# Scores of odd attention blocks in the banks of the first layer's products, seven weight-splitting pieces after step 12, attention's pools closed before the first layer's rest

## The chip, the cores and the metric

The kernel runs on one core of one Trainium2 chip. The time is device microseconds of one execution. The engines named below are TensorE (PE in the rows, its weight loads PEld), VectorE (DVE), ScalarE (ACT), GpSimd (POOL) and SyncE (SP), which issues the transfers. [...]

## What is computed

A chain of three parts. Attention with a local window of 32 positions and 32 global tokens; a first feed-forward layer (three weight matrices, the maximum over the three products, then an output matrix); and a layer of eight experts, each token going to one. Cut to what matters here:

```python
s_g = scale * q_g @ k_all.T;  out_g = softmax(s_g) @ v_all             # global queries see all
s_l = concat(scale * q_l @ k_g.T, where(|i - j| <= 32, scale * q_l @ k_l.T, -1e9))
out_l = softmax(s_l) @ concat(v_g, v_l)
x = concat(out_g, out_l)                                               # 1152 x 512
h = max(max(x @ w1, x @ w2), x @ w3)                                   # w: 512 x 768
x2 = h @ w_out
# then gate, argmax, and out[i] = gate_i * (relu(x2[i] @ W1[e]) @ W2[e])
```

## The kernel before

Attention is cut into 16 sets of two blocks, 32 blocks n of 128 queries and two heads each. A loop over steps s = -2 ... 37 runs them as a pipeline; each step does a little of several blocks. `SEQ` is the order inside a step (its first string for s < 14, its second from 14 on):

- `scores` (`u_scores(s + 2)`, L179): sixteen small matmuls into the tile `s`, two PSUM banks; `ps_s` has one such pair. In steps 1, 5, 9, 13 ... `glob` (`g_scores`, L257) writes the global queries' scores beside them, and `gcopy` (L272) copies those out.
- `max` (`u_max`, L193, on DVE): adds the mask, takes row maxima `nm` and leaves the masked scores in SBUF as `sm`. After it the pair of banks may be written again.
- `exp` (`u_exp`, L198, on ACT), `trans` (L212, `pt`, then ACT's copy `ph`, L217), `pv` (L226, `pv`, then DVE's `xq`, L228), `out` (L234, `pxq`, ACT's copy `xs`, L237, and POOL's split into `xh` and `xl`, L239 and L240). There is one bank each for `pt`, `pv` and `pxq`, so block n's product is written only after `xq` of block n - 1.
- `w0`, `w1`, `w2`: pieces of `w_stream`, the splitting of the float64 weights (18 tiles of 128 x 512 for the first layer, 6 of `w_out`) into two fp32r halves. A tile is seven pieces: ACT `ca` (L337), DVE `ca` (L339), `ca` (L342), `ct` (L345), ACT `wh` (L349), DVE `ca` (L352), DVE `ca` (L354) with POOL's two operations for `wl` (L355, L356); the next tile's load is issued along with them. `w_steps` is the number of pieces in a step: with nw pieces, `w0` gets nw // 3, `w1` (nw + 1) // 3 and `w2` (nw + 2) // 3.
- `idle`: `warm` matmuls on zeros (L88), which compute nothing; `idles` gives their number in a step. Each call takes a bank of `ps_mm`.
- `m0` ... `m3`: matmuls of the first layer (L455), pulled from `moe_stream` in the order of the table `ORDER` (window of tokens, slice of 128 of the 768 columns, and from which step on). A product is 12 matmuls into one bank of `ps_mm`, which has three; `part` then takes it out with ACT (L440), or with DVE, which keeps a running maximum `hA` (L442).

After the loop the rest of `moe_stream` runs with one piece of splitting behind every fifth matmul (the "rest" below). Then attention's pools are closed, and the banks that they held go to new pools: `BANKS`, the list that products rotate through, becomes six banks instead of three, and from there on `split64` keeps its scratch `a` in PSUM (`cap` in the rows instead of `ca`). Then come the other slices of the first layer, `w_out`, and the experts.

The instructions of each engine run in the order in which this code writes them. A set's queries and keys are a load of 320 KB, its values 512 KB, a tile of weights 512 KB, all in one queue of SP.

Of the kernel before, what the change touches and what calls it, by code (L numbers as in the profile page):

```python
# [7 lines left out]
F32 = mybir.dt.float32  # L8
# [6 lines left out]
ALU = mybir.AluOpType  # L15
# [4 lines left out]
P = 128  # L20
# [30 lines left out]
def tile_block(ctx: ExitStack, tc: tile.TileContext, qk, qg, v, vo, vg, w123, w_out, w_gate, w1, w2, consts, out):  # L51
    nc = tc.nc
# [18 lines left out]
    ps_mm = ctx.enter_context(tc.tile_pool(name="ps_mm", bufs=3, space=PSUM))  # L71
# [3 lines left out]
    ps_s = att.enter_context(tc.tile_pool(name="ps_s", bufs=1, space=PSUM))  # L75
# [17 lines left out]
    SS, raws, K, V, VG, W, SG_, PV_, PS_, PT_, SM, hT, GS = {}, {}, {}, {}, {}, {}, {}, {}, {}, {}, {}, {}, {}  # L93
# [76 lines left out]

    def u_scores(n):
        m, u = divmod(n, 2)
        ps = ps_s.tile([P, 2, 512], F32, tag="s", name=f"s{n}")
        PS_[n] = ps
        for j in range(2):
            t = K[m][64 * j : 64 * j + 64]
            for g in range(4):
                a = 256 + 32 * (5 * u + g)
                nc.tensor.matmul(ps[32 * g : 32 * g + 32, j, 0:P], lhsT=t[:, u * P + 32 * g : u * P + 32 * g + 32], rhs=t[:, a : a + P], start=True, stop=True)  # L179

    def u_max(n):
        m, u = divmod(n, 2)
        half = SETS[m][1]
        mk = mask[:, 0 if half == 0 and u == 0 else (2 if half == 1 and u == 1 else 1), :]
        nm = ap.tile([P, 2], F32, tag="nm", bufs=4, name=f"nm{n}")
        if u == 0:
            SS[m] = ap.tile([P, 2, 4], F32, tag="ssum", bufs=3, name=f"ss{m}")
        ssum = SS[m][:, 0, 2 * u : 2 * u + 2]
        sm = sms[n % NSM]
        SM[n] = (sm, nm, ssum)  # L190
        ps = PS_[n]
        for j in range(2):
            nc.vector.tensor_tensor_reduce(sm[:, j], ps[:, j, 0:P], mk, scale=-0.125, scalar=3.0e38, op0=ALU.add, op1=ALU.min, accum_out=nm[:, j : j + 1])  # L193

    def u_exp(n):
        sm, nm, ssum = SM[n]
# [46 lines left out]
    def g_scores(m):  # L243

        b, half, hp = SETS[m]
        quad = hp // 2
        if half == 0:
            SG_[b, quad] = ap.tile([P, S], F32, tag=f"sg{quad}", bufs=2, name=f"sg{b}{quad}")
        ps = PS_[2 * m + 3]
        n = 256 + 32 * half  # L250
        GS[m] = [ps[64 * j : 64 * j + 64, j, P : P + n] for j in range(2)]

        def part(out, cols):
            for a in range(2):
                for j in range(2):
                    r = slice(64 * j, 64 * j + 64)
                    nc.tensor.matmul(out(GS[m][j][32 * a : 32 * a + 32]), lhsT=QG[b][r, hp + a, 32 * j : 32 * j + 32], rhs=cols(K[m + a][r, 288:608]), start=True, stop=True)  # L257

        for s in range(2):
            part(  # L260
                lambda o: o[:, 0:256].rearrange("p (u s c) -> p u s c", u=2, s=2)[:, :, s],
                lambda k: k.rearrange("p (u c) -> p u c", u=2)[:, :, 96 * s : 96 * s + 64],
            )
        if half == 1:
            part(lambda o: o[:, 256:288], lambda k: k[:, 64:96])

    def g_copies(m):
# [309 lines left out]
    ws = w_stream()  # L577
# [2 lines left out]

    WIN1 = [(0, 256), (256, 256), (512, 288), (800, 288)]

    ORDER = [(0, 0, 13), (1, 0, 18), (0, 1, (20, 24, 26)), (2, 0, 27), (1, 1, 27), (2, 1, 27), (0, 2, (35, 35, 36)), (3, 0, 99), (1, 2, 99), (2, 2, 99), (3, 1, 99), (3, 2, 99)]

    def moe_stream():
        for g, f, at in ORDER:
            at = at if isinstance(at, tuple) else (at,) * 3
# [18 lines left out]

    SEQ = ('m3 scores glob max gcopy m2 w0 trans m1 pv out w1 recip quad exp w2 m0 idle', 'w0 trans scores glob max pv out gcopy idle exp w1 m3 m0 quad recip m1 m2 w2')
    GDVE = 6
    MM = ((3, 2, 1, 1), (7, 4, 2, 1))

    w_steps = {1: 1, 2: 2, 3: 2, 4: 2, 5: 2, 6: 2, 7: 2, 8: 2, 9: 2, 10: 3, 11: 3, 12: 2, 13: 1, 14: 1, 15: 2, 16: 2, 17: 1, 18: 2, 19: 2, 20: 2, 21: 2, 22: 2, 23: 2, 24: 2, 25: 2, 26: 2, 27: 3, 28: 2, 29: 2, 30: 3, 31: 3, 32: 3, 33: 3, 34: 2, 35: 2, 36: 2, 37: 2}
    idles = {-2: 4, 0: 1, 2: 1, 4: 3, 6: 1, 7: 1, 8: 1, 9: 2, 10: 1, 11: 1}

    GQ = {17: (0, 0), 21: (0, 1), 28: (1, 0), 31: (1, 1)}
    globs = []
    mstream = None
# [6 lines left out]
    for s in range(-2, NU + 6):  # L623
        live, ahead = 0 <= s < NU, 0 <= s + 2 < NU
        if s == 10:
            mstream = Stream(moe_stream())
        pull = (lambda n: mstream.pull(n, s)) if mstream else (lambda n: None)
        nw = w_steps.get(s, 0)
        for c_ in SEQ[0 if s < 14 else 1].split():
# [27 lines left out]
            elif c_[0] == "m" and c_ != "max":  # L657
                pull(MM[s > 26][int(c_[1])])

        if s % 2 == 0:  # L660
            m = (s + 8) // 2
# [9 lines left out]
            routing_start()  # L671
        if s == 30:
            nc.sync.dma_start(out.rearrange("(p i) (j c) -> p (i j) c", p=64, c=P), zero[0:64].unsqueeze(1).to_broadcast([64, NT * DM // 64 // P, P]))
    k = 0
    while mstream.next is not None:
        mstream.pull(1, 100)
        k += 1
        if mstream.next is not None and k % 5 == 0:
            take(ws, 1)
    flush()  # L680
    att.close()
    s2 = phl.enter_context(tc.tile_pool(name="s2", bufs=1))
    ps_x = ctx.enter_context(tc.tile_pool(name="ps_x", bufs=2, space=PSUM))
# [666 lines left out]
```

## Time and profile before

| what | value |
|---|---|
| median of three runs | 324.5 us (323.12 to 324.73) |
| the profiled execution, its own time | 324.16 us |
| its span, first to last instruction | 322.4 us, 1.8 us less than its time |
| TensorE busy | 306.5 us, 95% of the span |
| VectorE busy | 236.8 us, 73% |
| ScalarE busy | 181.6 us, 56% |
| GpSimd busy | 148.4 us, 46% |
| mean granted TensorE clock | 0.994 of full speed |

Busy shares are averages over stages with different limits. A time in the rows is counted from the first instruction of the span. In a row of the timeline the bracket at the end is the time that the engine sat idle before that instruction, and what ended it.

### The profile page before, as it was taken

What the parts mean: (1) busy time and instruction counts of PE and PEld (TensorE: products, weight loads), DVE (VectorE), ACT (ScalarE), POOL (GpSimd) and SP (SyncE); (2) the same over time, 40 slices, a digit from 0 to 9 for tenths busy, and PEclk for the clock granted to TensorE, in tenths of its full rate; (3) what the DMA queues carried; (4) which work ended last, traced back from release to release, by engine and by line L of the source; (5) the groups of instructions that cost most, each with busy time, mean ns of one, the idle gap of its engine ahead of it and who ended that gap; (6) DMA issues with size and microseconds to landing.
All of it is one profiled execution on the core that took longest, in us unless ns stands there. A gap on an engine that the chain in (4) does not pass through costs nothing. (4 is left out here: it accounts for less than half of the span.)

```text
span 322.4 us, 8727 instructions
## 1 busy us (share of the span) xinstructions
PE 306.5 (95%) x3284; PEld 260.8 (81%) x3284; DVE 236.8 (73%) x600; ACT 181.6 (56%) x457; POOL 148.4 (46%) x164
## 2 busy tenths in 40 slices
PE   7977998999999989999999999999999999999984
PEld 2544786778999989899999999999898778888852
DVE  2699577868887999999951004756787999999871
ACT  4876988786753333444331121348331789889851
POOL 1267746677694767788672000140000448731131
PEclk9999899999999999999999999999999999999999
DMA  7999887644972323332000030588564299999920
GB/s 256 412 404 401 312 297 266 234 147 149 198 201 67 103 95 93 106 130 67 0 3 0 2 130 2 176 309 323 206 212 182 79 365 399 393 403 399 383 67 22
DMA packets 27655, 64.42 MB, mean 200 GB/s; under 512 B 3018, under 2 KB 8140, under 8 KB 27600
## 3 DMA queue, kind: packets, MB, share of 16 engines
q1 hardware_dynamic: 26304, 59.91, 53.2%
q0 software_dynamic: 1296, 3.82, 3.3%
q8 instruction: 30, 0.49, 0.6%
q14 instruction: 25, 0.20, 0.2%
HBM read 60.95 MB, written 7.27 MB: 212 GB/s over the span
## 5 line engine op out<-in xcount | busy, mean ns | idle before, releaser
L455 PE MATMUL h<-xh,wh 128*128 128x256 f32 (+1 forms) x288 | 85.2, 296 | 1.7 <-DVE hA L442 1.7
L455 PE MATMUL h<-xl,wh 128*128 128x256 f32 (+1 forms) x288 | 84.3, 293 | 0.0
L455 PE MATMUL h<-xh,wl 128*128 128x256 f32 (+1 forms) x288 | 84.1, 292 | 0.0
L455 PEld LDWEIGHTS h<-xh,wh 128*128 128x128 f32 x288 | 54.9, 191 | 3.2 <-DVE hA L442 3.0
L455 PEld LDWEIGHTS h<-xh,wl 128*128 128x128 f32 x288 | 54.7, 190 | 0.6 <-issue 0.5
L455 PEld LDWEIGHTS h<-xl,wh 128*128 128x128 f32 x288 | 54.8, 190 | 0.2
L445 POOL TENSOR_TENSOR hTl<-hA,hTh 128x256 fp32r<-128x256 f32 (+1 forms) x24 | 20.4, 850 | 55.8 <-ACT hTh L444 55.8
L239 POOL CAST xh<-xs 128x128 fp32r<-128x128 f32 x32 | 14.9, 466 | 30.7 <-ACT xs L237 30.6
L749 PE MATMUL x<-hTl,wo_h 128*128 128x256 f32 (+1 forms) x96 | 28.3, 294 | 0.0
L869 DVE TENSOR_TENSOR w2l<-rawb,w2h 128x1024 fp32r<-128x1024 f32 x23 | 27.2, 1216 | 1.4 <-ACT w2h L868 1.4
L198 ACT ACTIVATE sm<-sm,nm 128x128 f32<-128x128 f32 x64 | 25.2, 398 | 4.9 <-DVE nm L193 4.8
L749 PE MATMUL x<-hTh,wo_l 128*128 128x256 f32 (+1 forms) x96 | 27.9, 291 | 0.0
L749 PE MATMUL x<-hTh,wo_h 128*128 128x256 f32 (+1 forms) x96 | 27.8, 289 | 0.0
L193 DVE CUSTOM_DVE_ANT_0 sm<-s,mask 128x128 f32<-128x128 f32 x64 | 16.0, 286 | 15.9 <-PE s L179 9.8
L442 DVE TENSOR_TENSOR hA<-hA,h 128x256 f32<-128x256 f32 (+1 forms) x48 | 20.6, 429 | 7.5 <-PE h L455 7.1
L356 POOL TENSOR_TENSOR wl<-ct,ca 128x512 fp32r<-128x512 f32 x18 | 24.7, 1370 | 2.6 <-DVE ca L354 1.4
L952 PE MATMUL py<-w2h,hhl 128*128 128x512 f32 x96 | 25.4, 395 | 0.2 <-DVE idsall L574 0.2
L869 DVE TENSOR_TENSOR w1l<-rawb,w1h 128x1024 fp32r<-128x1024 f32 x20 | 23.7, 1216 | 1.8 <-ACT w1h L868 1.7
L355 POOL TENSOR_TENSOR ct<-ct,wh 128x512 f32<-128x512 f32 x18 | 24.5, 1363 | 0.0
L349 ACT CAST wh<-ct 128x512 fp32r<-128x512 f32 x18 | 11.1, 617 | 21.9 <-DVE ct L345 21.6
L868 ACT CAST w2h<-rawb 128x1024 fp32r<-128x1024 f32 x23 | 23.3, 1048 | 0.2 <-DMA rawb<-in_w_dram 0.2
L827 POOL DMA_INDIRECT xg<-x2d,idsall x7 | 14.9, 2123 | 16.2 <-PE xp L839 15.0
(232 smaller groups left out, 719.1 us busy)
## 6 DMA issues: line engine op xcount, KB each, us to landing
rawb<-in_w_dram SPq DMA_DIRECT2D x51, 512.0 KB
raww<-in_w_dram SPq DMA_DIRECT2D x18, 512.0 KB
rawv<-in_v_dram SPq DMA_DIRECT2D x16, 512.0 KB
qk<-in_qk_dram SPq DMA_DIRECT2D x16, 320.0 KB
rawo<-in_w_out_dram SPq DMA_DIRECT2D x6, 512.0 KB
rw<-in_w_dram SPq DMA_DIRECT2D x5, 512.0 KB
out_dram<-zero SPq DMA_DIRECT2D x1, 2176.0 KB
rawg<-in_vo_dram SPq DMA_DIRECT2D x4, 512.0 KB
```

The lines of the kernel that those rows point to most:

```text
L193: nc.vector.tensor_tensor_reduce(sm[:, j], ps[:, j, 0:P], mk, scale=-0.125, scalar=3.0e38, op0=ALU.add, op1=ALU.min, accum_out=nm[:, j : j ...
L198: nc.scalar.activation(sm[:, j], sm[:, j], AF.Exp, bias=nm[:, j : j + 1], scale=-1.0, accum_out=ssum[:, j : j + 1])
L239: nc.gpsimd.tensor_copy(dst[0], xs)
L355: nc.gpsimd.tensor_tensor(tf, tf, hi.bitcast(F32), op=ALU.subtract)
L356: nc.gpsimd.tensor_tensor(lo, tf, b.bitcast(F32), op=ALU.add)
L442: nc.vector.tensor_tensor(hA[:, :T], hA[:, :T], ph[:, :T], op=ALU.max)
L445: nc.gpsimd.tensor_tensor(hl[:, f_, c0 : c0 + T], hA[:, :T], dst.bitcast(F32), op=ALU.subtract)
L455: nc.tensor.matmul(ph[:, :T], lhsT=w_[:, a], rhs=x_[:, c, c0 : c0 + T], start=n == 0, stop=n == 11)
L749: nc.tensor.matmul(po[:, :T], lhsT=w_[:, f, d * P : (d + 1) * P], rhs=h_[:, f_, c0 : c0 + T], start=k == 0, stop=k == 17)
L868: nc.scalar.copy(h_, raw_of(j, k))
L869: nc.vector.tensor_tensor(l_, raw_of(j, k), h_.bitcast(F32), op=ALU.subtract)
L952: nc.tensor.matmul(py[0:nt], lhsT=a[:, c, a0 : a0 + nt], rhs=w_[:, c], start=i == 0, stop=i == 23)
```

## The change

Three edits. Odd blocks below `ODD` = 14 get their scores in two single banks of `ps_mm` instead of the pair in `ps_s`; even blocks, and all from 14 on, stay in `ps_s`. The pieces of steps 1 to 12 fall from 25 to 18 and those of steps 13 to 23 rise by the same seven, with `idles` and the first entry of `ORDER` altered to go with it. And the rest of `moe_stream` runs after attention's pools are closed, in the six banks, without a `flush` between.

```diff
     def u_scores(n):
         m, u = divmod(n, 2)
-        ps = ps_s.tile([P, 2, 512], F32, tag="s", name=f"s{n}")
+        if n % 2 and n < ODD:
+            ps = [ps_mm.tile([P, 512], F32, tag="mm", name=f"s{n}{j}") for j in range(2)]
+        else:
+            s2_ = ps_s.tile([P, 2, 512], F32, tag="s", name=f"s{n}")
+            ps = [s2_[:, j] for j in range(2)]
...
-    ORDER = [(0, 0, 13), (1, 0, 18), ...
+    ORDER = [(0, 0, (13, 14, 17)), (1, 0, 18), ...
...
+    ODD = 14
...
-    w_steps = {1: 1, 2: 2, 3: 2, 4: 2, 5: 2, 6: 2, 7: 2, 8: 2, 9: 2, 10: 3, 11: 3, 12: 2, 13: 1, 14: 1, 15: 2, 16: 2, 17: 1, 18: 2, 19: 2, ...
-    idles = {-2: 4, 0: 1, 2: 1, 4: 3, 6: 1, 7: 1, 8: 1, 9: 2, 10: 1, 11: 1}
+    w_steps = {1: 1, 2: 1, 3: 1, 4: 1, 5: 1, 6: 2, 7: 1, 8: 2, 9: 2, 10: 2, 11: 2, 12: 2, 13: 2, 14: 3, 15: 3, 16: 2, 17: 2, 18: 2, 19: 3, ...
+    idles = {-2: 4, 0: 1, 2: 1, 4: 2, 6: 1, 8: 1, 9: 1, 10: 1, 11: 1, 12: 1, 13: 1}
...
-    k = 0
-    while mstream.next is not None:
-        mstream.pull(1, 100)
-        k += 1
-        if mstream.next is not None and k % 5 == 0:
-            take(ws, 1)
-    flush()
     att.close()
...
     WIN2 = [(0, 256), (256, 288), (544, 256), (800, 288)]
     k = 0
+    while mstream.next is not None:
+        mstream.pull(1, 100)
+        k += 1
+        if mstream.next is not None and k % 5 == 0:
+            take(ws, 1)
     for f in range(NF1, NF):
```

TensorE's order in step 10 and at the start of step 11, before (`s` scores, `pt` transposed weights, `pv` product, `pxq` transposed output; a bracket names the engines whose semaphores the instruction waits for):

```order
L179 MATMUL s_646<-qk_394 32x128 [waits DMAHW2_49,DVE_49,PE_49]
L179 MATMUL s_646<-qk_394 32x128 x7
L212 MATMUL pt_664<-cst,sm_125 128x128 [waits Activation_49]
L212 MATMUL pt_664<-cst,sm_125 128x128
L226 MATMUL pv_669<-rawv_307,ph_618 32x64 [waits DVE_49]
L226 MATMUL pv_669<-rawv_307,ph_618 32x64 x7
L234 MATMUL pxq_680<-cst,xq_629 128x128 [waits Activation_49]
L88 LDWEIGHTS idle
L88 MATMUL warm<-idle 32x512
L179 MATMUL s_697<-qk_394 32x128 [waits DVE_49,PE_49]
L179 MATMUL s_697<-qk_394 32x128 x7
```

The same place now:

```order
L183 MATMUL s_641<-qk_392 32x128 [waits DMAHW2_49]
L183 MATMUL s_641<-qk_392 32x128 x7
L216 MATMUL pt_654<-cst,sm_125 128x128 [waits Activation_49]
L216 MATMUL pt_654<-cst,sm_125 128x128
L230 MATMUL pv_659<-rawv_307,ph_611 32x64 [waits DVE_49]
L230 MATMUL pv_659<-rawv_307,ph_611 32x64 x7
L238 MATMUL pxq_670<-cst,xq_622 128x128 [waits Activation_49]
L88 LDWEIGHTS idle
L88 MATMUL warm<-idle 32x512 [waits PE_49]
L183 MATMUL s_688<-qk_392 32x128 x4
L183 MATMUL s_689<-qk_392 32x128 x4
```

The scores no longer wait for VectorE in either step; the next instruction that does is the product `pv`.

VectorE's order from the middle of step 10 to `xq` of step 11, before (an ISA row is a maximum; `ca` and `ct` are pieces of splitting):

```order
L354 SCALAR_TENSOR_TENSOR ca<-raww_155,ca 128x512
L228 TENSOR_TENSOR xq_678<-pv_669,ss_460 128x128
L339 TENSOR_SCALAR ca<-ca 128x512
L206 RECIPROCAL ss_552<-ss_552 128x4
L342 TENSOR_SCALAR ca<-ca 128x512
L193 ISA sm_125,nm_706<-s_697,mask 128x128
L193 ISA nm_706 128x1
L193 ISA sm_125,nm_706<-s_697,mask 128x128
L193 ISA nm_706 128x1
L345 SCALAR_TENSOR_TENSOR ct<-raww_261,ca 128x512
L228 TENSOR_TENSOR xq_725<-pv_716,ss_552 128x128
```

The same place now:

```order
L232 TENSOR_TENSOR xq_668<-pv_659,ss_456 128x128
L346 TENSOR_SCALAR ca<-ca 128x512
L210 RECIPROCAL ss_544<-ss_544 128x4
L349 SCALAR_TENSOR_TENSOR ct<-raww_155,ca 128x512
L197 ISA sm_125,nm_698<-s_688,mask 128x128
L197 ISA nm_698 128x1
L197 ISA sm_125,nm_698<-s_689,mask 128x128
L197 ISA nm_698 128x1
L232 TENSOR_TENSOR xq_715<-pv_706,ss_544 128x128
```

Two pieces instead of four stand here, and none between the maxima and `xq`.

VectorE's order in the rest of `moe_stream`, before (`hA` with `h` is the running maximum that frees a bank of a product):

```order
L339 TENSOR_SCALAR ca<-ca 128x512
L342 TENSOR_SCALAR ca<-ca 128x512
L442 TENSOR_TENSOR hA_512_2327<-hA_512_2327,h_512_1_2348 128x288
L345 SCALAR_TENSOR_TENSOR ct<-raww_2167,ca 128x512
L442 TENSOR_TENSOR hA_512_2327<-hA_512_2327,h_512_2_2370 128x288
L352 TENSOR_SCALAR ca<-ct 128x512
L354 SCALAR_TENSOR_TENSOR ca<-raww_2167,ca 128x512
```

The same place now:

```order
L343 TENSOR_SCALAR cap<-cap 128x512
L346 TENSOR_SCALAR cap<-cap 128x512
L446 TENSOR_TENSOR hA_512_2362<-hA_512_2362,h_512_1_2383 128x288
L349 SCALAR_TENSOR_TENSOR ct<-raww_2167,cap 128x512
L356 TENSOR_SCALAR cap<-ct 128x512
L446 TENSOR_TENSOR hA_512_2362<-hA_512_2362,h_512_2_2404 128x288
L358 SCALAR_TENSOR_TENSOR ca<-raww_2167,cap 128x512
```

The scratch of the pieces is in PSUM (`cap`) here; it was in SBUF.

## Rows read from the trace of the kernel before

**Rows 1.** Stretch; busy us (instructions) of PE, PEld, DVE, ACT, POOL; clock; DMA share; GB/s.

```profile
5.00:20.00 15.00, 12.99 (x302) 7.07 (x300) 10.13 (x54) 12.05 (x51) 3.94 (x9) 1.00 1.02 397
20.00:33.70 13.70, 10.84 (x225) 5.90 (x223) 12.85 (x43) 9.57 (x40) 11.01 (x16) 0.92 1.03 401
```

**Rows 2.** Timeline of TensorE, 0 to 40 us: start, duration, instruction, idle before.

```profile
6.63 0.45 PE L179 MATMUL s<-qk 64*32 64x128 f32 x16 [0.72 <-DVE nm L193]
...
10.20 0.45 PE L179 MATMUL s<-qk 64*32 64x128 f32 x16 [0.74 <-DVE sg L272]
...
13.26 0.45 PE L179 MATMUL s<-qk 64*32 64x128 f32 x16
...
14.62 0.82 PE L88 MATMUL warm<-idle 128*32 128x512 bf16 x3
15.37 0.45 PE L179 MATMUL s<-qk 64*32 64x128 f32 x16
...
16.19 0.44 PE L212 MATMUL pt<-cst,sm 128*128 128x128 f32 x2
...
17.73 0.45 PE L179 MATMUL s<-qk 64*32 64x128 f32 x16 [0.48 <-PE pxq L234]
...
24.11 0.45 PE L179 MATMUL s<-qk 64*32 64x128 f32 x16 [1.24 <-DVE nm L193]
...
29.52 0.43 PE L226 MATMUL pv<-rawv,ph 128*32 128x64 f32 x16 [0.40 <-DVE xq L228]
...
31.72 0.68 PE L179 MATMUL s<-qk 64*32 64x128 f32 x16 [1.20 <-issue]
...
33.66 0.56 PE L455 MATMUL h<-xh,wh 128*128 128x256 f32 x1
```

**Rows 3.** Timeline, 18 to 36 us, VectorE's rows of pieces.

```profile
22.17 1.37 DVE L342 TENSOR_SCALAR ca<-ca 128x512 int32<-128x512 int32 x1
...
31.54 0.88 DVE L345 SCALAR_TENSOR_TENSOR ct<-raww,ca 128x512 int32<-128x512 int32 x1
```

**Rows 4.** The same timeline, GpSimd and VectorE in step 9.

```profile
21.93 1.33 POOL L356 TENSOR_TENSOR wl<-ct,ca 128x512 fp32r<-128x512 f32 x1
...
25.58 0.92 DVE L272 COPY sg<-s 64x288 f32<-64x288 f32 x2
```

**Rows 5.** Five microseconds around the first layer's start, columns as in Rows 1.

```profile
30.00:35.00 5.00, 3.80 (x62) 2.31 (x66) 4.43 (x15) 2.77 (x10) 3.52 (x6) 0.66 1.01 391
```

**Rows 6.** One microsecond of that stretch, columns as in Rows 1.

```profile
32.00:33.00 1.00, 1.00 (x22) 0.34 (x10) 1.00 (x4) 0.54 (x2) 0.92 (x2) 0.50 0.96 373
```

**Rows 7.** Timeline, 0 to 40 us, ScalarE: the first exponential of steps 3 and 4.

```profile
13.61 0.41 ACT L198 ACTIVATE sm<-sm,nm 128x128 f32<-128x128 f32 x1
...
15.04 0.41 ACT L198 ACTIVATE sm<-sm,nm 128x128 f32<-128x128 f32 x1
```

**Rows 8.** Timeline of VectorE, 34 to 62 us.

```profile
44.93 0.29 DVE L193 CUSTOM_DVE_ANT_0 sm<-s,mask 128x128 f32<-128x128 f32 x1 [1.34 <-PE s L257]
...
46.70 1.79 DVE L354 SCALAR_TENSOR_TENSOR ca<-raww,ca 128x512 f32<-128x512 uint32 x1
```

**Rows 9.** Timeline of TensorE, 40 to 62 us.

```profile
49.06 0.68 PE L179 MATMUL s<-qk 64*32 64x128 f32 x16 [0.42 <-DVE nm L193]
```

**Rows 10.** Busy time in the rest of `moe_stream` and after it, columns as in Rows 1.

```profile
110.00:115.00 5.00, 4.42 (x35) 4.20 (x33) 4.79 (x7) 1.29 (x4) 3.81 (x3) 1.00 0.33 105
...
135.00:140.00 5.00, 5.00 (x42) 5.00 (x42) 4.87 (x10) 2.52 (x6) 3.92 (x4) 1.00 0.37 129
```

**Rows 11.** Timeline of TensorE, 106 to 133 us: two of its four stalls there.

```profile
114.90 0.40 PE L455 MATMUL h<-xh,wh 128*128 128x288 f32 x1 [0.57 <-DVE hA L442]
...
129.64 0.39 PE L455 MATMUL h<-xh,wh 128*128 128x256 f32 x1 [0.53 <-DVE hA L442]
```

**Rows 12.** One piece by the place of its scratch: ns min/median/max, first and last start.

```profile
L342 DVE TENSOR_SCALAR ca<-ca x16: 414/1018/1402, 14.7 to 127.8; 128x512 int32<-128x512 int32 x16
L342 DVE TENSOR_SCALAR cap<-cap x8: 693/700/700, 133.8 to 162.7; 128x512 int32<-128x512 int32 x8
```

More of the change, by code (lines that the diff above doesn't have):

```diff
@@ L178, in u_scores @@
                 a = 256 + 32 * (5 * u + g)
-                nc.tensor.matmul(ps[32 * g : 32 * g + 32, j, 0:P], lhsT=t[:, u * P + 32 * g : u * P + 32 * g + 32], rhs=t[:, a : a + P], start=True, stop=True)
+                nc.tensor.matmul(ps[j][32 * g : 32 * g + 32, 0:P], lhsT=t[:, u * P + 32 * g : u * P + 32 * g + 32], rhs=t[:, a : a + P], start=True, stop=True)
     def u_max(n):
@@ L192, in u_max @@
         for j in range(2):
-            nc.vector.tensor_tensor_reduce(sm[:, j], ps[:, j, 0:P], mk, scale=-0.125, scalar=3.0e38, op0=ALU.add, op1=ALU.min, accum_out=nm[:, j : j + 1])
+            nc.vector.tensor_tensor_reduce(sm[:, j], ps[j][:, 0:P], mk, scale=-0.125, scalar=3.0e38, op0=ALU.add, op1=ALU.min, accum_out=nm[:, j : j + 1])
     def u_exp(n):
@@ L250, in g_scores @@
         n = 256 + 32 * half
-        GS[m] = [ps[64 * j : 64 * j + 64, j, P : P + n] for j in range(2)]
+        GS[m] = [ps[j][64 * j : 64 * j + 64, P : P + n] for j in range(2)]
         def part(out, cols):
@@ L581, in tile_block @@
     WIN1 = [(0, 256), (256, 256), (512, 288), (800, 288)]
-    ORDER = [(0, 0, 13), (1, 0, 18), (0, 1, (20, 24, 26)), (2, 0, 27), (1, 1, 27), (2, 1, 27), (0, 2, (35, 35, 36)), (3, 0, 99), (1, 2, 99), (2, 2, 99), (3, 1, 99), (3, 2, 99)]
+    ORDER = [(0, 0, (13, 14, 17)), (1, 0, 18), (0, 1, (20, 24, 26)), (2, 0, 27), (1, 1, 27), (2, 1, 27), (0, 2, (35, 35, 36)), (3, 0, 99), (1, 2, 99), (2, 2, 99), (3, 1, 99), (3, 2, 99)]
     def moe_stream():
@@ L608, in tile_block @@
     GDVE = 6
+    ODD = 14
     MM = ((3, 2, 1, 1), (7, 4, 2, 1))
-    w_steps = {1: 1, 2: 2, 3: 2, 4: 2, 5: 2, 6: 2, 7: 2, 8: 2, 9: 2, 10: 3, 11: 3, 12: 2, 13: 1, 14: 1, 15: 2, 16: 2, 17: 1, 18: 2, 19: 2, 20: 2, 21: 2, 22: 2, 23: 2, 24: 2, 25: 2, 26: 2, 27: 3, 28: 2, 29: 2, 30: 3, 31: 3, 32: 3, 33: 3, 34: 2, 35: 2, 36: 2, 37: 2}
-    idles = {-2: 4, 0: 1, 2: 1, 4: 3, 6: 1, 7: 1, 8: 1, 9: 2, 10: 1, 11: 1}
+    w_steps = {1: 1, 2: 1, 3: 1, 4: 1, 5: 1, 6: 2, 7: 1, 8: 2, 9: 2, 10: 2, 11: 2, 12: 2, 13: 2, 14: 3, 15: 3, 16: 2, 17: 2, 18: 2, 19: 3, 20: 2, 21: 2, 22: 2, 23: 3, 24: 2, 25: 2, 26: 2, 27: 3, 28: 2, 29: 2, 30: 3, 31: 3, 32: 3, 33: 3, 34: 2, 35: 2, 36: 2, 37: 2}
+    idles = {-2: 4, 0: 1, 2: 1, 4: 2, 6: 1, 8: 1, 9: 1, 10: 1, 11: 1, 12: 1, 13: 1}
     GQ = {17: (0, 0), 21: (0, 1), 28: (1, 0), 31: (1, 1)}
```

## The prediction

> **What bounds the kernel now.** I read the busy time by stretch first, because the mean shares hide the stages. From 5 to 33.7 us, before the first product of the first layer, TensorE is busy 23.8 of 28.7 us [rows 1]: it is not the bound, and 4.9 us of it are gaps. VectorE is busy 10.1 of 15.0 us in the first half and 12.85 of 13.7 in the second, so it is the bound from 20 us on. The transfers run without a pause at some 400 GB/s in both halves, with a DMA share above 1. Then the timeline of TensorE shows where the gaps are [rows 2]. Six stand before the first product, 0.72 + 0.74 + 0.48 + 1.24 + 0.40 + 1.20 = 4.78 us. Four of them, named or by their place, end with VectorE having read the one pair of score banks: scores of the next block may not be written until the maxima (or the copies of the global scores) of the one before are out. The 0.48 us wait is put down to TensorE itself, but stands behind copies in the same way, and the 0.40 is a product that waits for VectorE's `xq`.
>
> Why the maxima are late is seen on VectorE and GpSimd: pieces of splitting stand ahead of them, and take 1.37 us where one was as short as 0.41 [rows 3, 12], while GpSimd runs its own 1.33 us operations [rows 4].
>
> From there to the end of the first layer TensorE is busy nearly all the time. The exception is the rest of `moe_stream`: 4.42 us busy of 5, with 35 matmuls, against 5.00 and 42 in a stretch after the pools were closed [rows 10]. The stalls end with VectorE's running maximum [rows 11], that is, with the freeing of a bank. So every microsecond of TensorE's that goes away before 135 us should come off the end.
>
> The sum below is made against the profiled execution's 324.16 us. It is 0.3 us under the median, which I take as no difference. A change under 0.5%, 1.6 us, is about what a measurement of this kernel can't tell from none.
>
> **First part: scores of odd blocks in two other banks, fewer pieces up to step 12.** Scores now wait only for the maxima of two blocks earlier. If every gap before the first product went, 4.78 us would. Two `warm` matmuls fewer stand in steps 0 to 12; three cost 0.75 us (14.62 to 15.37), so this gives 0.4, the first of a step costing more than the next. [...] Upper bound of this part up to the first product: 4.78 + 0.4 + 0.6 = 5.8.
>
> It won't be all. TensorE is in order, and two instructions behind the scores stands the product `pv`, which needs VectorE's `xq` of the block before; `xq` stands behind that step's maxima. So a gap is moved back by the scores and one transpose (0.75 us, and about 0.4 more where global scores are computed: 15.37 to 16.19 is 0.82, plain scores alone last 0.45). Where VectorE is over a step behind, it stalls there. I add up VectorE for the worst place, from the maxima of step 9 to `xq` of step 11. Maxima are 0.5 a step (two of 0.29 that overlap, [rows 8]); I take `xq`, of the same size, at 0.3 of these. The copies of the global scores are 0.92 [rows 4]. Of the four pieces, two behind GpSimd's work for the first tile take up to 1.37, and two 0.7 to 0.9 [rows 3]. That is 3 x 0.5 + 3 x 0.3 + 0.9 + about 4 = 7.3 us. TensorE has 1.36 a step (13.26 to 14.62), 0.5 more in step 9, which computes the longer global scores, 0.3 of `warm` in each of three steps and 0.75 before the product of step 12: 6.2 us, and VectorE starts 0.9 behind it. So 7.3 + 0.9 - 6.2 = 2.0 us of stall come back, or 1.2 if the pieces meet less of GpSimd's work. I take 1.6: 5.8 - 1.6 = **4.2 us**. Lower bound: only the four gaps of 0.72, 0.74, 1.24 and 1.20 go, 3.9 us, and 2.0 come back: 1.9.
>
> ScalarE is not in the way: 1.43 us a step (13.61 to 15.04, [rows 7]) is close to TensorE's 1.36, but it stood idle a fifth of the first half and more of the second [rows 1].
>
> **Second part: the clock behind the first product.** Without the long gaps I expect full clock, so the other **0.6 us** go. Lower bound 0: the dip comes anyway.
>
> **Third part: seven pieces more in steps 13 to 23.** They are about one tile: five operations of VectorE (0.42 to 1.79 us each, [rows 3, 8]), two of ScalarE, two of GpSimd (1.33). From step 14 all scores use the one pair again, so a late maximum stalls scores as before; behind them in TensorE's queue stand `pv`, `pxq` and seven matmuls of the first layer. VectorE had idle time of about 1 us a step there, as the 1.34 us ahead of a maximum shows [rows 8]. But 1.79 us pieces did make one late: scores waited 0.42 [rows 9]. In steps 14, 15, 19 and 23 a third piece now stands ahead of the maxima. Nothing lost is the lower bound; four waits of 1.24, the longest in the first stage, are the upper, 5.0. I take three waits of 0.42, the case nearest in kind: **1.3 us** given back. The later readiness of the third tile costs nothing: its second half follows within step 15, and `ORDER` asks for it from step 17.
>
> **Fourth part: six banks for the rest of `moe_stream`.** Between 110 and 130 us TensorE stalls four times, 0.57, 0.29, 0.34 and 0.53, of which two are shown [rows 11]: 1.7 us, the lower bound. By matmuls it is 35 in place of 42 in five us [rows 10], 0.83 us in each of four such stretches: 3.3, the upper bound, as some records may be missing. I take the middle, **2.5 us**. It needs VectorE to keep up: that was 4.79 of 5 us busy with three banks. In the stretch with six banks it was 4.87 busy with TensorE never idle, so it can, just.
>
> The scratch of the pieces goes to PSUM in this stage. In SBUF the same piece took 0.41 to 1.40 us, in PSUM 0.69 to 0.70 every time [rows 12], below the 1.02 median. [...] The new SBUF tiles lie over attention's, whose last readers are done by about 100 us, before this stage's first product is taken out; hence no wait is costed. If one came, it would delay ScalarE's first copy, with three more banks to run into meanwhile.
>
> **Sum:** 4.2 + 0.6 - 1.3 + 2.5 = 6.0 us; 324.2 - 6.0 = **318.2 us**.
>
> **Rivals.**
> *VectorE remains the bound of the first stage.* The stalls then move whole from the scores to `pv`. For it: 12.85 of 13.7 us busy [rows 1]. Against it: five operations fewer by step 12, and 4.9 us of VectorE's idle time in the first half. First part 1.9 instead of 4.2: 320.5 us. Chance 0.17.
> *The clock still falls.* [...] Both terms of 0.6 fail: 319.4 us. [...] Chance 0.12.
> *Transfers end the gain.* The loads ahead of set 4's keys are 4.8 MB, 12.1 us at 397 GB/s, so with the start of the first ones they land at about 14.6 us (an estimate); the scores that need them ran at 17.73, so 3.1 us may be gained by there. My path gains 2.2 by then. If the loads bind, the first part ends near 3.1: 319.3 us. Chance 0.06.
> *Slower: the maxima of steps 13 to 23 come late.* With one pair of banks, each loses its stall whole, and nothing takes it up later. It decides from 0.66 us in each of eleven steps, 7.3 in all (the 6.0 and my 1.3). At 0.9, between the 0.42 and the 1.24 seen, it is 9.9 us: 326.8. Against it stands VectorE's idle time there. Chance 0.05.
> *All goes well.* No late maximum behind step 13, and 3.3 us in the rest: 316.1. Chance 0.09.
>
> **How the numbers follow.** My forecast has the other 0.51. Around it the terms' bounds give 316.5 to 320.0. To leave out no more than 2 in 10 the range reaches to the cases on either side, with some more above for two of them together and below for a first part near its bound of 5.8: 315.0 to 322.0. Faster by over 0.5% are all cases but the slower one and mixtures of two: 0.89. Within: 0.06. Slower: 0.05.
>
> **What would show it.** First product of the first layer at 29 to 30 us instead of 33.66; scores of odd blocks below 14 without a wait for VectorE; remaining gaps at `pv` in steps 10 to 12. No stretch at half clock. The sum of TensorE's stalls between that product and the end of the loop grows by about 1.3 us. In the rest, 41 or 42 matmuls in each five us. I am wrong if scores still wait (then the banks rotate onto unread ones), if the product starts early but the loop ends no earlier, or if something behind the first layer takes up what TensorE gained.

## The result, and the profile after

The change made the kernel faster: 319.59 us median (319.11 to 321.87, six runs) against 324.03 (323.12 to 325.26, six runs beside it), a ratio of 0.9866 with an interval of [0.9834, 0.9898]. The forecast was 318.2 in a range of 315.0 to 322.0. The profiled execution took 319.86 us, its span is 318.1.

The total hides how it came about. This table is made from the starts of TensorE's instructions in the two traces (the first layer has 864 matmuls, counted from 0; the loop's end lies near the 288th, the rest of `moe_stream` ends at the 468th; `w_out` has 288):

| stretch | before, us | after, us | difference | forecast |
|---|---|---|---|---|
| start to first product | 33.66 | 31.21 | -2.45 | -4.2 |
| first product to 288th matmul | 72.80 | 74.71 | +1.91 | -0.6 + 1.3 |
| 288th to 468th matmul | 26.40 | 22.96 | -3.44 | -2.5 |
| 468th to the last of `w_out` | 94.53 | 94.53 | 0 | 0 |
| from there to the span's end | 95.0 | 94.7 | -0.3 | 0 |

Busy time by stretch of the kernel after (columns: stretch, its length, then busy us and instructions of PE, PEld, DVE, ACT and POOL, granted clock, DMA share, GB/s) answers to [rows 1, 5, 10]:

```profile
5.00:20.00 15.00, 13.64 (x301) 7.17 (x300) 8.54 (x53) 11.57 (x52) 3.35 (x9) 1.00 1.03 398
20.00:33.70 13.70, 12.76 (x287) 7.79 (x287) 11.21 (x48) 11.60 (x48) 10.01 (x16) 1.00 1.03 401
30.00:35.00 5.00, 4.73 (x99) 3.37 (x103) 3.73 (x18) 4.82 (x20) 4.25 (x7) 1.00 1.03 395
110.00:115.00 5.00, 5.00 (x41) 5.00 (x40) 4.48 (x9) 2.14 (x5) 3.76 (x4) 1.00 0.47 166
135.00:140.00 5.00, 5.00 (x42) 5.00 (x41) 4.68 (x9) 2.21 (x5) 4.14 (x5) 1.00 0.34 105
```

VectorE is no longer full ahead of the first product (11.21 of 13.7 us, it was 12.85), the granted clock of 30 to 35 us is 1.00 (it was 0.66), and in the rest TensorE is busy all 5.00 us, with 41 matmuls.

The timeline of TensorE (start, duration, instruction, idle before it and what ended it) answers to [rows 2, 9]:

```profile
14.04 0.45 PE L183 MATMUL s<-qk 64*32 64x128 f32 x16 [1.18 <-DMA qk<-in_qk_dram]
...
30.27 0.43 PE L230 MATMUL pv<-rawv,ph 128*32 128x64 f32 x16 [0.92 <-DVE xq L232]
...
31.21 0.39 PE L459 MATMUL h<-xh,wh 128*128 128x256 f32 x1
...
44.41 0.45 PE L183 MATMUL s<-qk 64*32 64x128 f32 x16 [0.61 <-DVE gnm L283]
...
54.12 0.33 PE L238 MATMUL pxq<-cst,xq 128*128 128x128 f32 x1 [0.40 <-ACT gph L301]
...
62.09 0.45 PE L183 MATMUL s<-qk 64*32 64x128 f32 x16 [0.73 <-PE pt L216]
```

No scores before the first product wait for VectorE any more. Two gaps of note remain there: one for the keys of set 3, one at the product `pv`. Behind it the gaps have grown: between the first product and the 288th matmul they add up to 3.72 us, where before had 2.24 (0.71 of that a single stop that waited for no data, at 56.26 us).

The piece with its scratch in PSUM (`cap`) and in SBUF (`ca`), min/median/max ns, answers to [rows 12]:

```profile
L346 DVE TENSOR_SCALAR cap<-cap x13: 699/700/700, 103.9 to 157.7; 128x512 int32<-128x512 int32 x13
L346 DVE TENSOR_SCALAR ca<-ca x11: 415/521/1382, 19.4 to 100.2; 128x512 int32<-128x512 int32 x11
```

### The profile page after: what moved, and what is told of

Same layout as the page of the kernel before. It is cut to its first block, busy times and chain, and to the rows that moved or that the text cites. A ratio compares the mean times of both kernels' runs of the same rounds, so it can differ in the third digit from the quotient of the medians.

```text
span 318.1 us, 8714 instructions
## 1 busy us (share of the span) xinstructions
PE 305.5 (96%) x3283; PEld 260.2 (82%) x3283; DVE 230.6 (73%) x600; ACT 182.9 (58%) x457; POOL 145.9 (46%) x164
## 5 line engine op out<-in xcount | busy, mean ns | idle before, releaser
L449 POOL TENSOR_TENSOR hTl<-hA,hTh 128x256 fp32r<-128x256 f32 (+1 forms) x24 | 19.5, 812 | 52.9 <-ACT hTh L448 52.9
L243 POOL CAST xh<-xs 128x128 fp32r<-128x128 f32 x32 | 13.5, 421 | 31.0 <-ACT xs L241 31.0
L360 POOL TENSOR_TENSOR wl<-ct,ca 128x512 fp32r<-128x512 f32 x18 | 24.0, 1333 | 2.7 <-DVE ca L358 1.4
L448 ACT CAST hTh<-hA 128x256 fp32r<-128x256 f32 (+1 forms) x24 | 10.1, 419 | 21.7 <-DVE hA L446 21.7
```

The lines of the kernel that those rows point to most:

```text
L360: nc.gpsimd.tensor_tensor(lo, tf, b.bitcast(F32), op=ALU.add)
L449: nc.gpsimd.tensor_tensor(hl[:, f_, c0 : c0 + T], hA[:, :T], dst.bitcast(F32), op=ALU.subtract)
```

## Experiments

The first question was which part the 4.4 us came from. The profiled execution is not always near the median: in odd alone, odd and fourth part, three banks, and pieces alone with two programs longer it is the slowest of the runs, so that medians decide on gains, and the traces only on where time goes. "Odd" stands for the odd scores in the products' banks, "pieces" for the moved pieces with `idles` and `ORDER`, "behind" for the rest running behind the closing of the pools. A ratio is that to the kernel before, run on the same chip, with its interval.

| kernel | odd | pieces | behind | six banks | scratch in PSUM | median, us | ratio |
|---|---|---|---|---|---|---|---|
| the change | yes | yes | yes | yes | yes | 319.59 | 0.9866 [0.9834, 0.9898] |
| fourth part alone | no | no | yes | yes | yes | 319.99 | 0.9882 [0.9859, 0.9904] |
| without the fourth part | yes | yes | no | no | no | 331.7 | 1.0227 [1.0204, 1.0251] |
| the same, GpSimd's program 8 longer | yes | yes | no | no | no | 323.85 | 1.0005 [0.9976, 1.0034] |
| odd alone | yes | no | no | no | no | 322.76 | 0.994 [0.9922, 0.9958] |
| pieces alone | no | yes | no | no | no | 336.29 | 1.0365 [1.0342, 1.0388] |
| the same, two programs longer | no | yes | no | no | no | 327.42 | 1.0097 [1.0069, 1.0125] |
| odd and fourth part | yes | no | yes | yes | yes | 319.74 | 0.9857 [0.9827, 0.9887] |
| scratch in SBUF | yes | yes | yes | yes | no | 319.51 | 0.9865 [0.9836, 0.9894] |
| three banks | yes | yes | yes | no | yes | 319.74 | 0.9868 [0.9836, 0.99] |
| neither | yes | yes | yes | no | no | 323.69 | 0.9995 [0.9976, 1.0015] |
| the change, keys first | yes | yes | yes | yes | yes | 319.39 | 0.9856 [0.9831, 0.9881] |
| odd, fourth part, keys first | yes | no | yes | yes | yes | 322.07 | 0.9942 [0.9916, 0.9968] |

**The fourth part alone.** Before, with only this moved (with it come six banks and the scratch in PSUM):

```diff
-    while mstream.next is not None:
-        mstream.pull(1, 100)
...
-    flush()
     att.close()
...
+    while mstream.next is not None:
+        mstream.pull(1, 100)
```

> The kernel before with the fourth part alone: the rest of the first layer's stream after attention's pools are closed, in six banks, with the scratch in PSUM. Theory A (the rest carries most of the change: in the two traces the 324th to 468th first-layer matmul took 3.4 us less, while everything ahead of the rest came only 0.5 us earlier): about 3.4 us off, 320.6 us, with 41 or more matmuls in each five us of the rest. Theory B (the prediction's terms: 2.5 here, 3.5 ahead of it): 321.5 us. Theory C (the rest gains only because the work ahead of it left fewer pieces): 323 us or more.

319.99 us, 0.9882: 1.18% of the whole change's 1.34%, a difference smaller than the half of either interval, and a little past theory A's 320.6. In its trace the 288th matmul starts at 105.96 (before 106.46, after 105.92) and the 468th at 128.91 (132.86, 128.88). Up to the 288th matmul this program is that of before, and yet it is as early there as the whole change: the 0.5 us by which the change leads at that place is no more than two executions of one program differ.

**Without the fourth part.** The change, with the loop put back ahead of `att.close()` and its `flush` behind it.

> The changed kernel without the fourth part: the rest runs before the pools are closed, in three banks. Theory A: only 0.5 us of the first stage's gain is left at the rest, so 323.5 us. Theory B: 3.5 us off, 320.5 us. By both, TensorE stalls in the rest again for bank releases, by 3 us or so.

331.7 us, outside both theories and far slower than before, which neither its first layer nor `w_out` explains: the last matmul of `w_out` starts at 228.10 (before 227.39), but from there to the end of the span it takes 102.7 us instead of 95.0. GpSimd's timeline shows where the loss begins:

```profile
255.34 1.92 POOL L964 DMA_INDIRECT out_dram<-y,ids  x1 [38.24 <-ACT w1h L873]
257.57 1.99 POOL L832 DMA_INDIRECT xg<-x2d,idsall  x1 [0.31 <-DVE w1l L874]
259.86 1.91 POOL L832 DMA_INDIRECT xg<-x2d,idsall  x1 [0.31 <-issue]
```

The scatter of `y` starts 3.0 us after `y` was written (251.66 + 0.69 us on ScalarE), where the run of odd alone, below, needed 0.85 (251.87 to 252.72). GpSimd's sequencer saw its wait end at 252.39 and issued the next instruction at 255.11. All the transfers of the stretch 252.4 to 255.1:

```profile
DMA packets 1, 0.01 MB, mean 3 GB/s; under 512 B 0, under 2 KB 0, under 8 KB 0
...
q14 instruction: 1, 0.01, 1.0%
```

One packet, of a queue named instruction, at 253.4. In the traces of before, after, the fourth part alone and odd alone the packet of that place comes at 212.7 to 223.5, some 28 us or more before the wait ends. What is late next: the two gathers now lie beside VectorE's splits (`w1l` and `w2l`, 255.15 to 262.04) and take 1.99 and 1.91 us, where those of odd alone took 1.05 and 1.35, so the second starts at 259.86 instead of 255.41 (odd alone); TensorE waits for its rows, which move beside the experts' weights (2.48 of the 3.33 MB between 257 and 267 us):

```profile
264.73 1.12 PE L844 MATMUL xp<-cst,xg 128*128 128x128 f32 x4 [5.69 <-DMA xg<-x2d,idsall]
```

Half clock, a granted clock of 0.50, from 262.8 to 269.6 (0.54 in the mean from 265 to 270) adds to it: the four matmuls `xp` took 1.12 us there, and 0.60 in the next run.

**The same with GpSimd's program eight instructions longer.**

```diff
     nc.gpsimd.memset(ones_b, 1.0)
+    for _ in range(8):
+        nc.gpsimd.memset(wg[:, 0, 0:1], 0.0)
```

> The change without its fourth part, with eight one-element memsets added to GpSimd's program near its start and nothing else. Without them this version took 331.7 us; it lost 8 us behind 228 us, where GpSimd, having waited 32 us for y, issued its next instruction only 2.72 us after the wait had ended (252.39 to 255.11), and one packet of the queue named instruction lies in that gap (253.4); in the other profiles that packet comes during the wait (212.7 to 223.5). Theory 1 (the program's text is fetched in blocks, and here a block ends just behind the waiting instruction): eight more instructions move the block's end ahead of the wait, the packet comes during it, and the time falls by about 8 us to 323 to 324 us, with a first scatter of y at about 253 us. Theory 2 (the moved pieces themselves make the tail late, by buffers or transfers): the memsets change nothing, 331 to 332 us.

323.85 us, as theory 1 had it. The packet lies at 214.2; how the program's text reaches the engine, which is that theory's reason, no run shows. GpSimd's rows are:

```profile
253.67 1.03 POOL L966 DMA_INDIRECT out_dram<-y,ids  x1 [36.10 <-ACT y L965]
255.00 1.05 POOL L834 DMA_INDIRECT xg<-x2d,idsall  x1 [0.30 <-DVE ordf L1227]
256.36 1.36 POOL L834 DMA_INDIRECT xg<-x2d,idsall  x1 [0.31 <-issue]
```

Eight useless instructions made the kernel 7.9 us faster by the medians, 7.2 by the two ratios. And with this out of the way the first three parts together give nothing that can be told from none: 1.0005 [0.9976, 1.0034].

**Odd alone, and pieces alone.** Before, once with `u_scores` and `ODD = 14` of the change, once with its `w_steps`, `idles` and `ORDER`.

> The kernel before with the scores of odd blocks up to 13 in the other banks alone; pieces, warm matmuls, order and the rest as before. If VectorE is the bound of the first stage, the stalls move from the scores to the product pv, and the first product of the first layer starts within 0.7 us of 33.66, with 324.0 us. If the single pair of banks was the bound, it starts at 31.5 or earlier, with 322 us or less.

> The kernel before with the new table of pieces, warm matmuls and order alone; scores all in the one pair, the rest as before. If pieces were what made the maxima late, the first product starts at 32 us or earlier, and the gain is mostly lost again by the rest: 323.5 us. If the pair of banks is what counts, the first product starts at 33 us or later, and the time is 324 to 325.5 us, since the seven pieces then cost 1 to 2 us behind step 12.

Odd alone gains 0.6%, between the two cases that I had expected, and a little over what can be told from none: in its profile the first product comes at 32.11, but the 288th matmul at 106.67 (before 106.46), with a stop of 1.79 us at 56.3 that the last section comes back to. That profile is of the slowest run, 323.94 us, so where the median's gain lies isn't shown. Pieces alone, 336.29 us, has the same 8 us behind `w_out` (its tail takes 102.7 us, the packet lies at 257.1), and loses 3.9 more by the 288th matmul; both theories missed it. TensorE's timeline shows two stops that no data explain, since they fall inside a group of sixteen equal matmuls:

```profile
26.46 0.42 PE L226 MATMUL pv<-rawv,ph 128*32 128x64 f32 x15
28.77 0.24 PE L226 MATMUL pv<-rawv,ph 128*32 128x64 f32 x1 [1.89 <-issue]
...
34.86 0.31 PE L226 MATMUL pv<-rawv,ph 128*32 128x64 f32 x4
36.61 0.42 PE L226 MATMUL pv<-rawv,ph 128*32 128x64 f32 x12 [1.44 <-issue]
```

The transfers from 26.2 to 27.4 hold one packet of the other queue of this name, among data packets that fill the engines:

```profile
q1 hardware_dynamic: 136, 0.46, 97.4%
q8 instruction: 1, 0.02, 5.6%
```

**Pieces alone, two programs longer.** Eight memsets on GpSimd as above, and on TensorE:

```diff
     warm(7)
+    tiny = ps_mm.tile([P, 512], F32, tag="mm", name="warm")
+    for _ in range(16):
+        nc.tensor.matmul(tiny[0:32, 0:32], lhsT=idle, rhs=idle, start=True, stop=True)
```

> The moved pieces alone, which took 336.3 us, with eight one-element memsets on GpSimd and sixteen matmuls of 32 columns on TensorE added near the start, where both wait for data. In the profile without them TensorE stood still for 1.89 and 1.44 us in the middle of a group of sixteen equal matmuls, and each time a packet of the queue named instruction had ended 1.4 us before; GpSimd stood still 2.7 us behind its long wait. Theory 1 (all three are late instruction text, and depend on where blocks end): 324.5 to 326 us, and no such gap. Theory 2 (only GpSimd's depends on that, TensorE's is due to the transfers, which take all their engines' time there): GpSimd's 8 us go, TensorE's gaps stay, 327.5 to 328.5 us. Theory 3 (the pieces themselves cost it): 335 to 336.5 us.

327.42 us: next to theory 2, 0.1 us below its range. GpSimd's 8 us went (its packet lies at 217.4). TensorE's stop did not go but came at another place, inside a pair of transposes:

```profile
25.85 0.33 PE L217 MATMUL pt<-cst,sm 128*128 128x128 f32 x1
27.23 0.33 PE L217 MATMUL pt<-cst,sm 128*128 128x128 f32 x1 [1.05 <-issue]
```

Half clock follows it, from 27.7 to 37.9 us, in this slowest of the five runs (mean granted clock 0.984; 0.995 to 0.998 in the others). So pieces alone cost some 3 us, of which gaps between first product and 288th matmul are one share, these stops and the clock another; they are not separated further.

**Odd and fourth part.** The change, with `w_steps`, `idles` and `ORDER` as before.

> Odd scores in the banks of the products and the six banks behind the attention, but the pieces and the idle matmuls where they were before. Theory A (what the first two parts gain up to the first product is taken up by the loop behind it, whatever the pieces do): as the whole change, 319.6 to 320.2 us, and the 288th matmul of the first layer again starts near 106.5 us. Theory B (the odd banks keep some of their gain, and the moved pieces give it away): the ratios of the two parts alone multiply, 0.994 x 0.988 = 0.982, so 318.2 to 318.7 us.

319.74 us, 0.9857: theory A by the median, but its interval reaches theory B's 0.982. The moved pieces are not needed; whether the odd banks add 0.2% to the fourth part's 0.9882 or nothing can't be told. The 288th matmul, which theory A had near 106.5, stands at 107.88 in the profile, the slowest run, with the stop of 1.79 us and 6.8 us at half clock ahead of it.

**Which half of the fourth part.** Three kernels, the change with `BANKS` or `PSA` or both set behind the rest instead of ahead of it (here for three banks):

```diff
-    BANKS[:] = [(ps_mm, "mm")] * 3 + [(ps_m4, "mm"), (ps_x, "px"), (ps_x, "px")]
     PSA.append(ps_y)
...  (the rest of moe_stream)
+    BANKS[:] = [(ps_mm, "mm")] * 3 + [(ps_m4, "mm"), (ps_x, "px"), (ps_x, "px")]
```

> The whole change, but the scratch of the pieces stays in SBUF while the rest of the first layer runs in six banks. Theory 'banks' (TensorE stalled there for a free bank, and three more take up the jitter of VectorE): nearly the whole gain stays, 319.6 to 320.4 us, 41 to 42 matmuls in each five us of 110 to 130. Theory 'scratch' (VectorE was the bound there, and gets faster by the pieces in PSUM): the gain of 3.4 us in that stage mostly goes, 322 to 323 us, 36 to 38 matmuls in each five us.

> The whole change, but the rest of the first layer keeps three banks, with the scratch of the pieces in PSUM. Theory 'banks': the gain of 3.4 us in that stage mostly goes, 322 to 323 us. Theory 'scratch': it stays, 319.6 to 320.4 us. Both needed: 321 to 322 us in both this run and the one with six banks and the scratch in SBUF.

> The control for the two halves of the fourth part: the whole change, the rest of the first layer stands behind the closing of attention's pools as there, but keeps its three banks and its scratch in SBUF. Theory 'either' (TensorE stalled because now and then a piece held VectorE too long for three banks; more banks or shorter pieces each end that): with neither, the four to six stalls come back, 288th to 468th matmul 26.4 to 26.9 us, 323.5 to 324 us. Theory 'moved' (the place of the loop alone did it, by other buffers or another order of VectorE's work): no stalls, about 22.95 us for that stage, 319.5 to 320 us.

I had expected one of the first two to lose the gain. Both keep all of it (319.51 and 319.74), and the stage takes 22.95 us in either; with neither it takes 26.96 us and the gain is gone (323.69). So it is "either". Busy time in the same stretch, first neither, then six banks with the scratch in SBUF, then three banks with it in PSUM:

```profile
120.00:125.00 5.00, 3.34 (x25) 3.10 (x24) 4.93 (x7) 1.09 (x3) 3.06 (x3) 1.00 0.31 105
```

```profile
120.00:125.00 5.00, 5.00 (x41) 5.00 (x40) 4.93 (x7) 1.19 (x3) 2.76 (x3) 1.00 0.28 105
```

```profile
120.00:125.00 5.00, 5.00 (x39) 5.00 (x39) 4.07 (x8) 2.33 (x5) 3.72 (x4) 1.00 0.26 105
```

VectorE is as busy in the first as in the second, 4.93 us with seven operations, while TensorE does 25 matmuls in one and 41 in the other. So VectorE goes at its own pace, and the question is what TensorE does when it gets ahead. VectorE's timeline with neither:

```profile
120.61 1.40 DVE L346 TENSOR_SCALAR ca<-ca 128x512 int32<-128x512 int32 x1
122.04 1.65 DVE L349 SCALAR_TENSOR_TENSOR ct<-raww,ca 128x512 int32<-128x512 int32 x1
123.61 0.44 DVE L446 TENSOR_TENSOR hA<-hA,h 128x288 f32<-128x288 f32 x1
...
126.42 1.40 DVE L346 TENSOR_SCALAR ca<-ca 128x512 int32<-128x512 int32 x1
```

Two pieces of 1.40 and 1.65 us stand next to each other ahead of the running maximum that frees a bank, and TensorE, which fills a bank in 1.5 us (15 products in 22.95), runs out of its three and stops:

```profile
124.10 0.41 PE L459 MATMUL h<-xh,wh 128*128 128x288 f32 x1 [1.66 <-DVE hA L446]
```

With six banks the same two pieces take as long, the next tile comes no sooner, and TensorE has no gap:

```profile
120.26 1.39 DVE L346 TENSOR_SCALAR ca<-ca 128x512 int32<-128x512 int32 x1
121.68 1.66 DVE L349 SCALAR_TENSOR_TENSOR ct<-raww,ca 128x512 int32<-128x512 int32 x1
123.26 0.44 DVE L446 TENSOR_TENSOR hA<-hA,h 128x288 f32<-128x288 f32 x1
...
126.08 1.40 DVE L346 TENSOR_SCALAR ca<-ca 128x512 int32<-128x512 int32 x1
...
129.10 0.44 DVE L446 TENSOR_TENSOR hA<-hA,h 128x288 f32<-128x288 f32 x1
```

With the scratch in PSUM they take 0.70 and 0.69, and three banks are enough:

```profile
121.10 0.70 DVE L346 TENSOR_SCALAR cap<-cap 128x512 int32<-128x512 int32 x1
121.89 0.69 DVE L349 SCALAR_TENSOR_TENSOR ct<-raww,cap 128x512 int32<-128x512 int32 x1
122.50 0.45 DVE L446 TENSOR_TENSOR hA<-hA,h 128x288 f32<-128x288 f32 x1
...
125.73 0.70 DVE L346 TENSOR_SCALAR cap<-cap 128x512 int32<-128x512 int32 x1
```

The rows show that the two cures differ. With the scratch in SBUF VectorE needs 5.5 to 5.8 us for the pieces of a tile and the maxima among them, up to 0.5 of it waiting for ScalarE's first piece, with three banks (120.61 to 126.42) as with six (120.26 to 126.08). A tile is seven pieces, one behind every fifth matmul, so 35 matmuls, and TensorE left alone does these in 4.5 us (180 in 22.95). VectorE's sum is too long, by about a microsecond a tile, and the two pieces in a row are only where TensorE's longest stop falls. Six banks don't mend that, they hold the backlog: with them the maximum of a product starts 0.8 us behind its last matmul just ahead of the stage, and 6.3 us behind it later (122.84 to 129.10), and of the 36 operations that VectorE has in this stage with the scratch in PSUM it has done 28 at the stage's end. The backlog is worked off behind the stage, where the scratch is in PSUM in every kernel. With the scratch in PSUM a tile takes 4.4 to 4.8 us, VectorE keeps up, and no maximum starts more than 0.8 us behind its product. That six banks would run full in a longer stage is to be expected from this, but was not run.

**Keys first.** The change, and odd with the fourth part, each with the keys of set 3 asked for ahead of the weights:

```diff
-    take(ws, 1)
     dma_qk(3)
     dma_v(2)
-    take(ws, 1)
+    take(ws, 2)
```

> The whole change, and the keys of set 3 and the values of set 2 are asked for ahead of the first two pieces' weights. In four of the five profiles with odd banks and early keys on time, scores of block 6 waited 0.8 to 1.3 us for set 3. Theory 'transfers' (that wait is part of why the first product came at 31.2 and not at 29.5): the wait goes, the product comes 0.5 to 1 us earlier, and 0.3 to 1 us of it stays: 318.6 to 319.3 us. Theory 'VectorE' (the product pv of step 11 waits for xq at 30.3 in any case, and pieces that start later make that wait longer): the wait moves there, 319.4 to 320 us.

> Odd banks and six banks with the pieces where they were before (319.7 us in an earlier run), and the early loads of the keys of set 3. The moved pieces cost 1.2 us of gaps between the scores of block 24 and the 288th matmul (1.9 against 0.56 to 0.8 us), so this should be the best version if the early loads help: 318.4 to 319.2 us. If VectorE's queue ahead of xq is what counts, then more pieces by step 12 keep the wait at pv, as in the run without early loads (0.85 and 1.41 us), and it gives 319.5 to 320 us.

In the first the wait of 1.18 us for set 3 is gone, but `pv` of step 11 waits longer, and the product comes only 0.4 us earlier; the median, 319.39, is no different from the change's.

```profile
29.87 0.43 PE L230 MATMUL pv<-rawv,ph 128*32 128x64 f32 x16 [1.29 <-DVE xq L232]
30.80 0.39 PE L459 MATMUL h<-xh,wh 128*128 128x256 f32 x1
```

The second I had taken for the best version; it is outside both forecasts and 2.3 us slower than without the edit (322.07 to 319.74, with intervals that don't meet). With the pieces early again, a piece of ScalarE now waits for its weights, and the copies `ph` that TensorE needs stand behind it:

```profile
14.24 0.66 ACT L341 ACTIVATE ca<-raww 128x512 f32<-128x512 f32 x1 [2.11 <-DMA raww<-in_w_dram]
...
14.80 0.35 ACT L221 COPY ph<-pt 128x256 f32<-128x256 f32 x1
...
15.21 0.44 PE L216 MATMUL pt<-cst,sm 128*128 128x128 f32 x2 [2.10 <-ACT ph L221]
```

Half clock follows, from 16.6 to 20.0 (and again from 33.7 to 40.5, with a granted clock of 0.57 between 33 and 41 us):

```profile
16.00:21.00 5.00, 5.00 (x79) 2.69 (x81) 3.47 (x15) 2.51 (x12) 1.72 (x4) 0.66 1.03 403
```

Here moving the pieces does pay: with them moved, the longest wait of this kind is 0.74 us, and no half clock follows (mean granted clock 0.998, against 0.984).

No version clearly beats the change; the fourth part alone is within 0.2% of it with one edit in place of three.

## Why the prediction was right, and where it was not

The median fell within the range and 1.4 us from the forecast, but by two errors of opposite sign, which is luck: the first three parts were to give 3.5 us and gave none that can be measured, the fourth was to give 2.5 and gave 3.8 (0.9882 of 324). One of the prediction's own signs of being wrong came true: the product starts 2.45 us earlier, and the loop ends hardly earlier. And its "316.5 to 320.0" from the terms' bounds doesn't follow from them: all upper bounds together give 314.5 us, all lower ones 325.6.

**First part, 4.2 us, mis-sized.** The mechanism was as told: scores no longer wait, the wait that remains is at `pv`, and it is 0.92 us, less than my 1.6. But 1.18 us went to the keys of set 3. That is the rival of the transfers, one set earlier than I had put it (set 4), and it was priced at 1.1 for the whole. Part of what is missing may be this execution's own, but that isn't shown: the trace's record of full clock begins at 6.75 us instead of 4.27, the four `warm` matmuls of step -2 took 1.89 us instead of 1.04, and scores of block 1 started at 6.48 instead of 5.46. In the run with the scratch in SBUF, with that record from 4.5 and 0.79 us for set 3, the first product stands at 30.68; in the run with neither cure, with the record as late as 6.8 but only 0.08 us for set 3, at 30.82. Neither came to the 29.5 of the forecast. Removing the wait for the keys didn't help, since `pv` took it up: near 30 us VectorE's queue ahead of `xq` decides.

**Second part, 0.6 us, can't be seen in the sum.** The dip behind the first product went. The sum has 0.6 us for the clock here and another 0.6 ahead of the first product, in the first part's 5.8; no run shows either term by itself. What the trace of before shows is a granted clock of 0.50 from 31.58 to 34.99 us, 2.1 us ahead of that product and 1.3 behind it. Without gaps and the `warm` matmul that now stands in step 13, the stretch from the first product to the 288th matmul is 72.80 - 2.24 = 70.56 us before, with 1.3 us at half clock in it, and 74.71 - 3.72 - 0.32 = 70.67 after, with none. That doesn't make half clock free. In four profiles with the moved pieces and no half clock there (after, scratch in SBUF, neither, keys first) the same difference is 70.7 to 70.9 us; with 2.7 and 2.9 us of it (the two kernels without the fourth part) it is 71.5 and 71.6. So half clock cost some 0.3 of its length (an estimate from these differences); the 2.1 us ahead of the product are then some 0.6 us and the 1.3 behind it some 0.4 (estimates), and the moved pieces took up that 0.4 too, in rows that read as busy.

**Third part, 1.3 us given back, mis-sized, and half of it at other places.** It was 1.91 net: 1.48 of gaps, 0.32 for the `warm` of step 13, which I hadn't counted. Without the stop of 0.71 us that before has there, the gaps grew by 2.1, and with the estimate for the clock the third part gave back more than 1.91. Two of the gaps are scores, as I had it (0.61 and 0.73); the others stand mostly at `pxq` (0.40, 0.29 and 0.33), behind ScalarE and VectorE.

So the step that failed is "every microsecond of TensorE's that goes away before 135 us should come off the end". The moved pieces are the same work, and cost behind the product about what had been gained ahead of it: 1.91 of the 2.45 us in the two traces, and odd alone gains 0.6% that odd with the pieces doesn't have. Where they are late can be seen in all nine profiles with the moved pieces: the stretch from the scores of block 24 to the 288th matmul has gaps of 1.80 to 1.93 us, against 0.56 to 0.84 without, and 1.37 in odd alone.

**Fourth part, 2.5 us, mis-sized.** It was 3.44 in the trace. I had taken the middle between the stalls shown (1.7) and the count of matmuls (3.3). The count was right: idle time understated this stage, because half of the loss lay inside rows that read as busy (1.74 us of gaps in before, 3.44 us of time). With the scratch in PSUM the piece took 0.699 to 0.700 us each time. What I had wrong is why VectorE would do: I read it off a stretch with six banks (4.87 us busy of 5), but the scratch lay in PSUM there. It is the scratch that lets VectorE keep up, and with it three banks are enough. With six banks and the scratch in SBUF VectorE falls behind by 6.3 us, and the banks hold that up to the stage's end.

**The clock.** No half clock in the stages of the profile of after that the change touches (its record reads 1.00 from 6.75 to 317.37 us), although gaps of 0.92 and 1.18 us remain. That is not assured: the run with three banks has the same program up to the rest, and its profile shows half clock at 14.5 to 18.0 and 31.6 to 38.4 and its 288th matmul at 109.46 instead of 105.92; it is the slowest of six runs, 323.07 us. Differences of a few us in the first stage are read from medians, not from one profile.

## What to carry to other kernels

When TensorE waits for an engine to free its banks, add up that engine's work for one round (here a tile: 5.8 us) and set it against TensorE's (4.5 us). Here it was longer. Shorter pieces (0.70 us instead of 1.40 and 1.65) were the cure; three banks more held the backlog (6.3 us) and did as well in a stage of 22.95 us, a longer one was not run. Count a stage's rate in matmuls per stretch, not in idle time alone (3.44 us lost here, 1.74 idle). And before believing that a variant is slower, see whether an engine stands still with nothing to wait for: here eight memsets more moved such a stop, worth 7.9 us against the change's 4.4.

## What the runs showed of the hardware

**GpSimd stood still behind a long wait.** Two of twelve experiments lost 8 us to a stop of 2.7 us. That the packet in the gap holds GpSimd's instructions is argued from its queue's name and place, and was not shown; that the stop goes away with a longer program of GpSimd is shown by the two runs with eight memsets more (323.85 us for 331.7, 327.42 for 336.29, with the packet at 214.2 and 217.4, ahead of the wait's end).

**TensorE had stops that look the same.** In the first layer and ahead of it, over all fourteen profiles, ten stops of 0.2 us or more, up to 1.89, stand with nothing to wait for: eight inside a group of equal instructions (one of them in the kernel before: 0.71 us at 56.26), and in two of the three kernels with odd banks and early pieces one of 1.79 us between `pv` and `pxq`, at 56.3 and 56.8. All ten end 1.33 to 1.54 us behind the end of a packet of the second instruction queue. Six more, of 0.23 to 1.68 us, stand behind 309 us, 1.43 to 1.85 us behind such a packet. That this is late program text is argued, as above, and was not shown. Sixteen small matmuls more in TensorE's program moved such stops without removing them (1.05 us at 27.23 where 1.89 at 28.77 and 1.44 at 36.61 had been), and of two kernels with the same program up to there one stood 0.60 us at 40.2 and the other 0.05. Why TensorE stops at these packets and not at the others is open: the transfers that fill their engines would fit the stops up to 40 us, not those at 56, where the DMA share is 0.3 to 0.5 (0.32 in before between 54 and 55 us). It also leaves open what odd banks with early pieces would be worth without theirs.
